# Reordering the passage, the batch change and every group of a fused attention and two-layer kernel

## The chip, the cores and the metric

One core of a Trainium2 chip. The metric is the device time of one execution in microseconds (us), the median over the runs that were timed. The engines are TensorE (PE in the profile, with PEld for its weight loads), VectorE (DVE), ScalarE (ACT), GpSimd (POOL) and SyncE (SP, which here issues the DMAs). Each runs its own instructions in the order in which they are written, and engines wait for one another by semaphores.

## What is computed

The reference, cut to what matters: masked attention, a first two-layer block with a squared ReLU, and a second block of four experts weighted for each token.

```python
mask = q_assign[:, :, :, None] == k_assign[:, :, None, :]
scores = np.where(mask, scale * np.matmul(q, k.transpose(0, 1, 3, 2)), -1e9)
attn = softmax(scores)                       # 2 batches, 8 heads, 768 x 768
x = np.matmul(attn, v)  ->  (1536, 512)
r = np.maximum(x @ w_in, 0.0)                # 512 -> 2048
x = (r * r) @ w_out                          # 2048 -> 512
p = domain_probs / (domain_probs.sum(-1, keepdims=True) + 1e-09)
for e in range(4):                           # 512 -> 1024 -> 512
    h = np.maximum(x @ w1[e], 0.0)
    out += p[:, e:e + 1] * (h @ w2[e])
```

Every operand of a product is held as a rounded part (`hi`) and a remainder (`lo`), and a product is three matmuls: hi by hi, hi by lo, lo by hi. So every weight and every activation is first rounded on ScalarE, and then its remainder is taken by a subtraction on VectorE or GpSimd.

## The kernel before

**Attention** fills the first 290 us of the profile and is not touched.

**The first block** runs over 48 iterations `n` = (4 chunks of 512 hidden columns) x (3 blocks of 512 tokens) x (4 tiles). Iteration `n` issues `gemm1(n)` (12 matmuls), `gemm2(n - 4)` (12 matmuls), and then what a list `plan` holds for slot `n`. ScalarE does ReLU, square and rounding of `gemm1`'s result (L636 to L638), GpSimd its remainder (L639). At the end of a block of tokens `gemm2`'s four banks are copied out by ScalarE (L653, first chunk) or added by VectorE (L655, later chunks). The slots of `plan` hold the conversions of the weights of coming chunks: five VectorE operations on the raw words (L161 to L177), then in the next slot the rounding on ScalarE (L183) and the remainder on VectorE (L185). `base` sets at which slot a chunk's conversions begin, `freed` when the raw buffer can be loaded again. The last slots prepare the second block: weight group 0 (`prep0`) and the first token operands.

**The second block** uses a Strassen-like scheme of 7 products for each 2 x 2 blocks. It runs over 32 groups `n`: 16 groups of 256 hidden columns (`NFQ`) for batch 0, and the same for batch 1. One group is 7 products (L756, 6 matmuls of 384 columns each) with 6 token tiles of the group before (L796, 6 matmuls of 512 columns each) between them. In each group:

- products 1, 6, 7 and 4 share PSUM bank A; before the next of them may write into it, ScalarE copies it out (`c_copy`, L767; product 6 waits for copy 0, product 7 for copy 1, product 4 for copy 2). Bank B or C is added to a copy on VectorE (`c_add`, L770).
- `h_hi` (ReLU and rounding, ScalarE, L776) and `h_lo` (remainder, VectorE, L779) make the operands of the next group's token tiles; VectorE adds each token tile's result to the output (L804, L806).
- `fq_prep(n + 1)` prepares the next group's weights in five steps: `sums` (four sums of 128x256 each, L715 to L718), `raws` and `mixed` (roundings L724, remainders L725), `second` (L742, L743), and the load of a later group.

**The token operands** are seven: RB11, RB21, RB22 straight from the first block's output, and RT1 to RT4, made of them by `t_sum` (L682). Each is rounded by `r_hi` (ScalarE, L685) and has its remainder by `r_lo` (VectorE or GpSimd, L688). For batch 0 this happens in **the passage** between the blocks, before group 0, and with the last `gemm2` calls put between group 0's products as `fill`. For batch 1 the four sums are all made in group 13, and the roundings and remainders in group 15, each after the product that used the old operand: **the batch change**.

The order on every engine is the order of this code; there is no scheduler.

Of the kernel before, what the change touches and what calls it, by code (L numbers as in the profile page):

```python
# [33 lines left out]
def moe_attention_kernel(  # L34
# [165 lines left out]
    with tc.manual_schedule():  # L200
# [502 lines left out]
        def fq_prep(n):  # L703
# [5 lines left out]
            def sums():  # L709
                w = st["r"] = raw_t["q", n][:, 0:1024].rearrange("p (k f) -> p k f", k=KD)  # L710
                a11, a12 = w[:, 0:2, 0:128], w[:, 2:4, 0:128]
                a21, a22 = w[:, 0:2, 128:256], w[:, 2:4, 128:256]
                s1, s2, s3, s4 = [mp["s"][:, k] for k in range(4)]
                sub = ALU.subtract
                nc.vector.tensor_tensor(s1, a21, a22, op=ALU.add)  # L715
                nc.vector.tensor_tensor(s3, a11, a21, op=sub)
                nc.vector.tensor_tensor(s2, s1, a11, op=sub)
                nc.vector.tensor_tensor(s4, a12, s2, op=sub)  # L718

# [24 lines left out]

            return [sums, raws, mixed, second, lambda: fq_load(n + 2)]

# [72 lines left out]
        for ci in range(NC1):  # L819
            base = 0 if ci == 0 else NF if ci == 1 else (ci - 1) * per  # L820
            for ci, part, half in w_loads(ci):
# [9 lines left out]
        for x in range(2):  # L831
            plan.append((freed[x - 2], 1, lambda x=x: fq_load(x)))
        prep0 = fq_prep(0)
        at0 = (NC1 - 1) * per
        for x, slot in ((0, at0), (1, at0 + 1), (2, at0 + 2), (3, at0 + LAG), (4, at0 + LAG)):
            plan.append((slot, 2, prep0[x]))
        plan.append((at0 + 2 * NF, 2, lambda: [r_hi(0, RB11), r_hi(0, RB21)]))
        plan.append((at0 + 2 * NF, 2, lambda: [r_lo(0, i, nc.gpsimd) for i in (RB11, RB21)]))
# [247 lines left out]
        for n in range(NEARLY, n1):  # L1086
# [6 lines left out]
                for k in range(2 * LAG)]  # L1093
        for i in (RT3, RT1):
            t_sum(0, i)
        r_hi(0, RT1)
        r_hi(0, RT3)
        t_sum(0, RT2)
        r_lo(0, RT1, nc.vector)
        r_hi(0, RT2)  # L1100
        r_lo(0, RT3, nc.gpsimd)
        t_sum(0, RT4)
        r_lo(0, RT2, nc.vector)
        r_hi(0, RT4)
        r_hi(0, RB22)
        r_lo(0, RB22, nc.gpsimd)
        r_lo(0, RT4, nc.vector)

        NN = 2 * NFQ
        for n in range(NN):  # L1110
            pb[n, "A"] = bank[n % 2]
            pb[n, "C"] = bank[2 + n % 2]
            pb[n, "B"] = bank[4] if n else bank[3]
            prep = fq_prep(n + 1)
            swap = n == NFQ - 1
# [6 lines left out]
            for x, i in enumerate(order):  # L1122
                product(n, i)
                if i == 1:
                    c_copy(n, 0)
                elif i == 6:
                    c_copy(n, 1)
                elif i == 2:
                    c_add(n, 0, "B")
                    h_hi(n, 0, 0)  # L1130
                elif i == 7:
                    c_copy(n, 2)
                elif i == 4:
                    h_hi(n, 1, 0)
                elif i == 3:
                    c_add(n, 1, "C")
                    h_hi(n, 0, 1)
                for f in fills[x]:
                    f()
                if i == 1 and n:  # L1140
                    h_lo(n - 1, 0, 1)
                elif i == 2:
                    h_lo(n, 0, 0)
                elif i == 7:
                    c_add(n, 2, "C")
                    h_hi(n, 1, 1)
                elif i == 4:
                    h_lo(n, 1, 0)
                    h_lo(n, 1, 1)
                if x < 5:  # L1150
                    prep[x]()
                if n == NFQ - 3 and x < 4:
                    t_sum(1, (RT3, RT1, RT2, RT4)[x])
                if swap:
                    r = PROD[i][1]
                    r_hi(1, r)
                    r_lo(1, r, nc.vector if x % 2 else nc.gpsimd)
        h_lo(NN - 1, 0, 1)
# [33 lines left out]
```

## Time and profile before

| | us |
|---|---|
| time, median of 3 runs | 1074.04 |
| lowest and highest run | 1072.1 and 1076.75 |
| the profiled execution | 1072.37 |
| span of its instructions | 1070.6 |
| TensorE busy | 1033.6 (97% of the span) |
| VectorE, ScalarE, GpSimd busy | 732.3, 538.2, 479.7 |

The profiled execution's time is 1.8 us above its span, and 1.7 us below the median of the runs. TensorE's busy time includes matmuls at the lower of its two clocks. A wait printed behind a row is the idle time of that engine just before the row, with the instruction that ended it.

### The profile page before, as it was taken

The numbers are of one execution on the slowest core, as the hardware profiler recorded it, in microseconds if no ns is written. First come the engines' busy times: TensorE is split into PE (matmuls) and PEld (weight loads), VectorE is DVE, ScalarE is ACT, GpSimd is POOL, SyncE is SP. The second block draws the span as 40 slices with busy tenths as digits, with TensorE's granted clock in tenths as the row PEclk, the third lists the DMA queues.
The fourth block names the chain that finished last, engine by engine and source line by source line (L and its number), as shares of the span: only waits on it lengthen the run. The fifth ranks groups of instructions, "written<-read, shape, count | busy, mean of one in ns | idle before, by whom it ended". The sixth has DMA issues, their size and how long they took to land.

```text
span 1070.6 us, 15323 instructions
## 1 busy us (share of the span) xinstructions
PE 1033.6 (97%) x5649; PEld 916.8 (86%) x5649; DVE 732.3 (68%) x1204; ACT 538.2 (50%) x1073; POOL 479.7 (45%) x465
## 2 busy tenths in 40 slices
PE   8899999998999999999989999999999999999998
PEld 7888888898887888888878888988888889989997
DVE  8698888787788873831156666666778666667664
ACT  6687887887655543434343333334344343333331
POOL 2467776665222222224343454444356454454440
PEclk9999999999999999999999999999999999999999
DMA  5766676873023230310002212211214212212201
GB/s 155 165 160 143 144 158 158 203 181 91 1 79 109 88 118 7 111 40 5 36 1 79 79 40 79 79 54 66 79 40 138 78 42 79 79 41 78 80 1 59
DMA packets 74651, 91.59 MB, mean 86 GB/s; under 512 B 27344, under 2 KB 50192, under 8 KB 74576
## 3 DMA queue, kind: packets, MB, share of 16 engines
q1 hardware_dynamic: 74576, 90.62, 29.7%
q8 instruction: 44, 0.72, 0.3%
q14 instruction: 31, 0.25, 0.1%
HBM read 59.83 MB, written 3.15 MB: 59 GB/s over the span
## 4 chain that ended last, share of the span: by engine, by line
PE 70%; DVE 6%; ACT 3%; DMA 2%; POOL 1%; issue 1%; SPq 0%; POOLq 0%; ACTq 0%
PE bank L796 23%; PE bank L756 20%; PE bank L649 10%; PE bank L631 3%; PE bank L632 3%; PE bank L630 3%; PE t L511 2%; PE s L478 1%; PE po L525 1%; PE po L527 1%; DVE ts L682 1%; PE m L377 1%; DVE x L806 1%; DMA q<-nql 0%; DVE fa L172 0%
## 5 line engine op out<-in xcount | busy, mean ns | idle before, releaser
L796 PE MATMUL bank<-w1h,ga 128*128 128x512 f32 x768 | 270.5, 394 | 0.0
L756 PE MATMUL bank<-xa,w0h 128*128 128x384 f32 x896 | 230.2, 338 | 8.4 <-ACT fa L767 8.4
L806 DVE SCALAR_TENSOR_TENSOR x<-bank,pe_p,x 128x512 f32<-128x512 f32 x180 | 134.7, 749 | 137.5 <-PE bank L796 137.5
L756 PEld LDWEIGHTS bank<-xa,w0h 128*128 128x128 f32 x896 | 164.9, 189 | 28.2 <-ACT fa L767 11.1
L796 PEld LDWEIGHTS bank<-w1h,ga 128*128 128x128 f32 x768 | 144.5, 188 | 24.6
L776 ACT ACTIVATE ga<-fa 128x384 fp32r<-128x384 f32 x96 | 50.4, 525 | 203.1 <-DVE fa L770 203.1
L796 PE MATMUL bank<-w1l,ga 128*128 128x512 f32 x384 | 151.9, 395 | 0.0
L756 PE MATMUL bank<-xa,w0l 128*128 128x384 f32 x448 | 150.5, 336 | 0.0
L639 POOL TENSOR_TENSOR ga<-fa,ga 128x512 fp32r<-128x512 f32 x48 | 63.0, 1313 | 189.7 <-ACT ga L638 132.6
L725 POOL TENSOR_TENSOR w0l<-raw,w0h 128x512 fp32r<-128x512 f32 x64 | 73.2, 1168 | 145.1 <-ACT w0h L724 145.1
L649 PE MATMUL bank<-ga,w1h 128*128 128x512 f32 x384 | 127.2, 391 | 2.2 <-ACT x L653 2.2
L517 DVE TENSOR_TENSOR ptl<-t,pth 128x384 fp32r<-128x384 f32 x192 | 99.1, 551 | 28.9 <-ACT pth L516 28.8
L725 POOL TENSOR_TENSOR w0l<-fa,w0h 128x1024 fp32r<-128x1024 f32 x32 | 77.3, 2415 | 76.2 <-ACT w0h L724 76.2
L487 DVE TENSOR_REDUCE nb<-s 128x1 f32<-128x768 f32 x96 | 91.2, 950 | 14.8 <-PE s L478 13.7
L767 ACT COPY fa<-bank 128x384 f32<-128x384 f32 x96 | 45.6, 475 | 105.2 <-PE bank L756 105.2
L516 ACT CAST pth<-t 128x384 fp32r<-128x384 f32 x192 | 83.1, 485 | 26.3 <-PE t L511 25.8
L743 POOL TENSOR_TENSOR w1l<-raw,w1h 128x1024 fp32r<-128x1024 f32 x32 | 85.4, 2668 | 21.5 <-ACT w1h L742 21.5
L511 PE MATMUL t<-identf,p 128*128 128x128 f32 x576 | 87.6, 279 | 6.3 <-DVE ptl L517 6.0
L498 ACT ACTIVATE p<-s,nb 128x768 f32<-128x768 f32 x96 | 87.5, 912 | 7.0 <-DVE nb L487 6.9
L478 PE MATMUL s<-k,q 80*128 80x384 f32 (+1 forms) x384 | 86.6, 346 | 2.7 <-DMA k<-ohm 2.5
L649 PEld LDWEIGHTS bank<-ga,w1h 128*128 128x128 f32 x384 | 72.5, 189 | 17.4 <-ACT x L653 2.6
L756 PEld LDWEIGHTS bank<-xa,w0l 128*128 128x128 f32 x448 | 84.7, 189 | 0.0
(180 smaller groups left out, 1997.1 us busy)
## 6 DMA issues: line engine op xcount, KB each, us to landing
raw<-in_moe_w_dram SPq DMA_DIRECT2D x64, 512.0 KB, 4.3
raw<-in_moe_w_in_dram SPq DMA_DIRECT2D x8, 1024.0 KB, 5.2
q<-nqh SPq DMA_DIRECT2D x42, 192.0 KB, 3.0
raw<-in_moe_w_out_dram SPq DMA_DIRECT2D x6, 1024.0 KB, 4.9
k<-nkh SPq DMA_DIRECT2D x28, 192.0 KB, 3.3
q<-nql SPq DMA_DIRECT2D x28, 192.0 KB, 3.7
nv<-in_v_dram SPq DMA_DIRECT2D x16, 192.0 KB, 3.7
out_dram<-x SPq DMA_DIRECT2D x12, 256.0 KB, 2.1
```

The lines of the kernel that those rows point to most:

```text
L478: nc.tensor.matmul(s[:, j, 0:HALF], stk[i, nq][:, t * 128:(t + 1) * 128], stk[i, nk][:, j * HALF:(j + 1) * HALF], start=first, stop=not first)
L487: nc.vector.tensor_reduce(out=nb, in_=s_ps[u][:, :, 0:HALF], axis=AX.XY, op=ALU.max, negate=True)
L498: nc.scalar.activation(p, s_ps.pop(u)[:, :, 0:HALF], AF.Exp, bias=nb_t.pop(u), accum_out=sums_t[hp][:, i % 2, t:t + 1])
L511: nc.tensor.transpose(tp[:, j], p_sb[u][:, half, j * 128:(j + 1) * 128], identf)
L516: return (lambda: nc.scalar.copy(dh, tp), lambda: nc.vector.tensor_tensor(dl, tp, dh.bitcast(F32), op=ALU.subtract))
L517: lambda: nc.vector.tensor_tensor(dl, tp, dh.bitcast(F32), op=ALU.subtract))
L649: nc.tensor.matmul(o, a, b, start=(ft == 0 and z == 0), stop=(ft == NF - 1 and z == 2))
L725: nc.gpsimd.tensor_tensor(v[1], src, v[0].bitcast(F32), op=ALU.subtract)
L743: nc.gpsimd.tensor_tensor(lo, w, hi.bitcast(F32), op=ALU.subtract)
L756: nc.tensor.matmul(ps, w[:, o:o + 128], r_op(r, x)[:, kt], start=(first and kt == 0 and z == 0), stop=(kt == 1 and z == 2), skip_group_che ...
L796: nc.tensor.matmul(o, a, w[:, f], start=(f == 0 and z == 0), stop=(f == 1 and z == 2))
L806: nc.vector.scalar_tensor_tensor(out=acc, in0=o, scalar=pc, in1=acc, op0=ALU.mult, op1=ALU.add)
```

## The change

No arithmetic is changed and TensorE's own order stays as it is. What other engines do is moved:

1. The conversions of chunks 1 to 3 of the first block begin two slots later.
2. The four weight sums of each group go from VectorE to GpSimd; `second` is issued before `mixed`.
3. `h_hi(n, 0, 0)` and `h_lo(n, 0, 0)` are issued after product 7 and its `c_copy`, no longer after product 2.
4. In the passage: the sums of group 1's weights are made before the passage, the token operands are written in a new order with part of them inside group 0's loop, their remainders all on VectorE, and the other preparation of group 1 begins at the third product.
5. The token sums of batch 1 are spread, one in each of groups 10 to 13. In group 15 the remainders are on GpSimd after the third and sixth product and else on VectorE (before: GpSimd and VectorE in turn, four and three).

```diff
-                nc.vector.tensor_tensor(s1, a21, a22, op=ALU.add)
-                nc.vector.tensor_tensor(s3, a11, a21, op=sub)
-                nc.vector.tensor_tensor(s2, s1, a11, op=sub)
-                nc.vector.tensor_tensor(s4, a12, s2, op=sub)
+                nc.gpsimd.tensor_tensor(s1, a21, a22, op=ALU.add)
+                nc.gpsimd.tensor_tensor(s2, s1, a11, op=sub)
+                nc.gpsimd.tensor_tensor(s3, a11, a21, op=sub)
+                nc.gpsimd.tensor_tensor(s4, a12, s2, op=sub)
...
-            return [sums, raws, mixed, second, lambda: fq_load(n + 2)]
+            return [sums, raws, second, mixed, lambda: fq_load(n + 2)]
...
-            base = 0 if ci == 0 else NF if ci == 1 else (ci - 1) * per
+            base = 0 if ci == 0 else NF + 2 if ci == 1 else (ci - 1) * per + 2
...
         prep0 = fq_prep(0)
+        prep1 = fq_prep(1)
         at0 = (NC1 - 1) * per
-        for x, slot in ((0, at0), (1, at0 + 1), (2, at0 + 2), (3, at0 + LAG), (4, at0 + LAG)):
+        for x, slot in ((0, at0), (1, at0 + 1), (3, at0 + 2), (2, at0 + LAG), (4, at0 + LAG)):
             plan.append((slot, 2, prep0[x]))
+        plan.append((at0 + LAG + 2, 2, prep1[0]))
...
-        for i in (RT3, RT1):
-            t_sum(0, i)
-        r_hi(0, RT1)
-        r_hi(0, RT3)
-        t_sum(0, RT2)
-        r_lo(0, RT1, nc.vector)
-        r_hi(0, RT2)
-        r_lo(0, RT3, nc.gpsimd)
-        t_sum(0, RT4)
-        r_lo(0, RT2, nc.vector)
-        r_hi(0, RT4)
-        r_hi(0, RB22)
-        r_lo(0, RB22, nc.gpsimd)
-        r_lo(0, RT4, nc.vector)
...
+        head = {
+            -1: [("t", RT3), ("t", RT1), ("h", RT1), ("t", RT2), ("l", RT1)],
+            0: [("h", RT2), ("h", RT3), ("t", RT4), ("l", RT2)],
+            1: [("l", RT3), ("h", RT4), ("h", RB22)],
+            2: [("l", RT4), ("l", RB22)]}
+        r_ops(0, head[-1])
...
                 elif i == 2:
                     c_add(n, 0, "B")
-                    h_hi(n, 0, 0)
                 elif i == 7:
                     c_copy(n, 2)
+                    h_hi(n, 0, 0)
...
-                elif i == 2:
-                    h_lo(n, 0, 0)
                 elif i == 7:
                     c_add(n, 2, "C")
+                    h_lo(n, 0, 0)
                     h_hi(n, 1, 1)
...
-                if x < 5:
-                    prep[x]()
-                if n == NFQ - 3 and x < 4:
-                    t_sum(1, (RT3, RT1, RT2, RT4)[x])
+                if n:
+                    if x < 5:
+                        prep[x]()
+                else:
+                    r_ops(0, head.get(x, []))
+                    if 2 <= x < 6:
+                        prep[x - 1]()
+                if x == 2 and 0 <= n - (NFQ - 6) < 4:
+                    t_sum(1, (RT3, RT1, RT2, RT4)[n - (NFQ - 6)])
                 if swap:
                     r = PROD[i][1]
                     r_hi(1, r)
-                    r_lo(1, r, nc.vector if x % 2 else nc.gpsimd)
+                    r_lo(1, r, nc.gpsimd if x in (2, 5) else nc.vector)
```

How this stands on the engines, at three places. First ScalarE in the first block's early iterations, before: the conversions' roundings (L183) stand between the steps of the iterations and ahead of the four copies L653.

```order
L183 CAST w0h<-cva 128x4x128
L636 ACTIVATE fa<-bank_4763 128x512
L637 ACTIVATE fa<-fa 128x512
L638 CAST ga<-fa 128x512
L183 CAST w0h<-fa 128x4x128
L636 ACTIVATE fa<-bank_4764 128x512
L637 ACTIVATE fa<-fa 128x512
L638 CAST ga<-fa 128x512
L653 COPY x_4769<-bank_4765 128x512
```

The same place after the change: the two roundings now come behind the copies.

```order
L636 ACTIVATE fa<-bank_4763 128x512
L637 ACTIVATE fa<-fa 128x512
L638 CAST ga<-fa 128x512
L636 ACTIVATE fa<-bank_4764 128x512
L637 ACTIVATE fa<-fa 128x512
L638 CAST ga<-fa 128x512
L653 COPY x_4769<-bank_4765 128x512
```

Second ScalarE in the passage, from RT1's rounding through group 0, before. `bank_4761` is bank A, `x_4769` and `ts` hold token operands, `w0h` and `w1h` group 1's weights.

```order
L685 CAST xa<-x_4769 128x768
L685 CAST xa<-ts 128x768 x3
L685 CAST xa<-x_4769 128x768
L767 COPY fa<-bank_4761 128x384
L776 ACTIVATE ga<-fa 128x384
L724 CAST w0h<-raw 128x512
L724 CAST w0h<-raw 128x256
L724 CAST w0h<-fa 128x1024
L767 COPY fa<-bank_4761 128x384
L742 CAST w1h<-raw 128x1024
L767 COPY fa<-bank_4761 128x384
```

After the change: the first copy stands behind one rounding in place of five, and no `h_hi` (L776) and no rounding of the weight sums (`fa`) stands ahead of the second copy.

```order
L685 CAST xa<-x_4769 128x768
L767 COPY fa<-bank_4761 128x384
L685 CAST xa<-ts 128x768 x3
L685 CAST xa<-x_4769 128x768
L724 CAST w0h<-raw 128x512
L724 CAST w0h<-raw 128x256
L767 COPY fa<-bank_4761 128x384
L742 CAST w1h<-raw 128x1024
L767 COPY fa<-bank_4761 128x384
L776 ACTIVATE ga<-fa 128x384 x2
L724 CAST w0h<-fa 128x1024
```

Third VectorE in one later group, from the second token tile's result on, before (L770 are the three `c_add`, L779 the `h_lo`).

```order
L806 SCALAR_TENSOR_TENSOR x_4769<-bank_4767,pe_p,x_4769 128x512
L806 SCALAR_TENSOR_TENSOR x_4769<-bank_4768,pe_p,x_4769 128x512
L770 TENSOR_TENSOR fa<-bank_4765,fa 128x384
L806 SCALAR_TENSOR_TENSOR x_4769<-bank_4766,pe_p,x_4769 128x512
L779 SCALAR_TENSOR_TENSOR ga<-fa,ga 128x384
L806 SCALAR_TENSOR_TENSOR x_4769<-bank_4767,pe_p,x_4769 128x2x256
L770 TENSOR_TENSOR fa<-bank_4763,fa 128x384
L806 SCALAR_TENSOR_TENSOR x_4769<-bank_4768,pe_p,x_4769 128x2x256
L779 SCALAR_TENSOR_TENSOR ga<-bank_4761,ga 128x384
```

After the change: the first `h_lo` has moved behind the second `c_add`, just ahead of the last token tile's result (the four sums ahead of these rows are gone).

```order
L806 SCALAR_TENSOR_TENSOR x_4769<-bank_4767,pe_p,x_4769 128x512
L806 SCALAR_TENSOR_TENSOR x_4769<-bank_4768,pe_p,x_4769 128x512
L770 TENSOR_TENSOR fa<-bank_4765,fa 128x384
L806 SCALAR_TENSOR_TENSOR x_4769<-bank_4766,pe_p,x_4769 128x512
L806 SCALAR_TENSOR_TENSOR x_4769<-bank_4767,pe_p,x_4769 128x2x256
L770 TENSOR_TENSOR fa<-bank_4763,fa 128x384
L779 SCALAR_TENSOR_TENSOR ga<-fa,ga 128x384
L806 SCALAR_TENSOR_TENSOR x_4769<-bank_4768,pe_p,x_4769 128x2x256
L779 SCALAR_TENSOR_TENSOR ga<-bank_4761,ga 128x384
```

## Rows read from the trace of the kernel before

**Rows 1.** The page's first part: busy us, share, instructions of each engine.
```profile
PE 1033.6 (97%) x5649; PEld 916.8 (86%) x5649; DVE 732.3 (68%) x1204; ACT 538.2 (50%) x1073; POOL 479.7 (45%) x465
```

**Rows 2.** TensorE's waits: us in total, times, longest.
```profile
PE bank L756 <- ACT fa L767: 8.4, 6, 3.4
```

**Rows 3.** TensorE's timeline, rows with a wait: start, us, idle before.
```profile
326.54 0.50 PE L649 MATMUL bank<-ga,w1h 128*128 128x512 f32 x1 [2.20 <-ACT x L653]
...
550.87 0.61 PE L756 MATMUL bank<-xa,w0h 128*128 128x384 f32 x2 [0.43 <-ACT fa L767]
557.02 0.97 PE L756 MATMUL bank<-xa,w0h 128*128 128x384 f32 x2 [3.43 <-ACT fa L767]
...
768.53 0.87 PE L756 MATMUL bank<-xa,w0h 128*128 128x384 f32 x2 [2.52 <-ACT fa L767]
...
803.04 0.62 PE L756 MATMUL bank<-xa,w0h 128*128 128x384 f32 x2 [1.41 <-ACT fa L767]
...
812.24 0.61 PE L756 MATMUL bank<-xa,w0h 128*128 128x384 f32 x2 [0.43 <-ACT fa L767]
...
820.03 0.62 PE L756 MATMUL bank<-xa,w0h 128*128 128x384 f32 x2 [0.23 <-ACT fa L767]
```

**Rows 4.** Windows: length, busy us (instructions) of each engine, granted clock, DMA.
```profile
557.09:560.50 3.41, 3.41 (x10) 3.12 (x11) 0.56 (x1) 1.33 (x3) 3.41 (x3) 0.50 0.00 0
560.50:563.91 3.41, 3.41 (x18) 3.02 (x17) 0.83 (x2) 1.00 (x2) 1.54 (x1) 1.00 0.17 44
768.71:772.13 3.42, 3.42 (x10) 3.10 (x11) 1.04 (x2) 1.01 (x2) 2.15 (x1) 0.50 0.02 6
```

**Rows 5.** ScalarE's timeline in the first block's iterations 6 to 8.
```profile
323.58 0.62 ACT L183 CAST w0h<-fa 128x512 fp32r<-128x512 f32 x1 [2.73 <-DVE fa L177]
...
325.91 2.04 ACT L653 COPY x<-bank 128x512 f32<-128x512 f32 x4
```

**Rows 6.** The passage, group 0: timelines of VectorE (first row) and ScalarE.
```profile
550.61 2.06 DVE L715 TENSOR_TENSOR fa<-raw 128x256 f32<-128x256 f32 x1
...
554.31 0.52 ACT L776 ACTIVATE ga<-fa 128x384 fp32r<-128x384 f32 x1 [3.49 <-DVE fa L770]
...
556.50 0.47 ACT L767 COPY fa<-bank 128x384 f32<-128x384 f32 x1
```

**Rows 7.** Groups 13 and 15: timelines of GpSimd, VectorE and ScalarE.
```profile
761.40 2.40 POOL L725 TENSOR_TENSOR w0l<-fa,w0h 128x1024 fp32r<-128x1024 f32 x1 [2.58 <-ACT w0h L724]
...
760.15 0.95 DVE L682 TENSOR_TENSOR ts<-x 128x768 f32<-128x768 f32 x1
...
761.68 2.94 DVE L682 TENSOR_TENSOR x<-x 128x768 f32<-128x768 f32 x1
...
766.64 0.52 ACT L776 ACTIVATE ga<-fa 128x384 fp32r<-128x384 f32 x1 [5.32 <-DVE fa L770]
...
797.76 1.05 ACT L724 CAST w0h<-fa 128x1024 fp32r<-128x1024 f32 x1 [1.81 <-DVE fa L718]
...
801.79 0.83 ACT L685 CAST xa<-x 128x768 fp32r<-128x768 f32 x1
```

**Rows 8.** Group 14, an undisturbed one: timelines of ScalarE, VectorE, GpSimd and TensorE.
```profile
780.24 1.05 ACT L724 CAST w0h<-fa 128x1024 fp32r<-128x1024 f32 x1
...
786.70 0.55 DVE L770 TENSOR_TENSOR fa<-bank,fa 128x384 f32<-128x384 f32 x1
...
788.47 0.75 DVE L806 SCALAR_TENSOR_TENSOR x<-bank,pe_p,x 128x512 f32<-128x512 f32 x1 [1.22 <-PE bank L796]
...
784.41 2.67 POOL L743 TENSOR_TENSOR w1l<-raw,w1h 128x1024 fp32r<-128x1024 f32 x1 [0.62 <-ACT w1h L742]
...
790.35 0.39 PE L796 MATMUL bank<-w1h,ga 128*128 128x512 f32 x1
```

**Rows 9.** GpSimd's cost: remainders of 512 and 256 columns, alone and over 31 groups.
```profile
555.41 1.95 POOL L725 TENSOR_TENSOR w0l<-raw,w0h 128x512 fp32r<-128x512 f32 x2 [3.02 <-ACT w0h L724]
...
L725 POOL TENSOR_TENSOR w0l<-raw,w0h 128x256 fp32r<-128x256 f32 x31 | 32.2, 1038 | 0.0
```

More of the change, by code (lines that the diff above doesn't have):

```diff
@@ L1093, in moe_attention_kernel, with r_ops @@
                 for k in range(2 * LAG)]
-        for i in (RT3, RT1):
-            t_sum(0, i)
-        r_hi(0, RT1)
-        r_hi(0, RT3)
-        t_sum(0, RT2)
-        r_lo(0, RT1, nc.vector)
-        r_hi(0, RT2)
-        r_lo(0, RT3, nc.gpsimd)
-        t_sum(0, RT4)
-        r_lo(0, RT2, nc.vector)
-        r_hi(0, RT4)
-        r_hi(0, RB22)
-        r_lo(0, RB22, nc.gpsimd)
-        r_lo(0, RT4, nc.vector)
+        def r_ops(b, ops):
+            for f, i in ops:
+                if f == "t":
+                    t_sum(b, i)
+                elif f == "h":
+                    r_hi(b, i)
+                else:
+                    r_lo(b, i, nc.gpsimd if f == "g" else nc.vector)
+        head = {
[4 more added lines that the diff above has]
+        r_ops(0, head[-1])
         NN = 2 * NFQ
@@ L1113, in moe_attention_kernel @@
             pb[n, "B"] = bank[4] if n else bank[3]
-            prep = fq_prep(n + 1)
+            prep = fq_prep(n + 1) if n else prep1
             swap = n == NFQ - 1
@@ L1149, in moe_attention_kernel @@
                     h_lo(n, 1, 1)
-                if x < 5:
-                    prep[x]()
-                if n == NFQ - 3 and x < 4:
-                    t_sum(1, (RT3, RT1, RT2, RT4)[x])
+                if n:
+                    if x < 5:
+                        prep[x]()
+                else:
+                    r_ops(0, head.get(x, []))
[3 more added lines that the diff above has]
+                    t_sum(1, (RT3, RT1, RT2, RT4)[n - (NFQ - 6)])
                 if swap:
```

## The prediction

> **What bounds the kernel now.** I read the page first: TensorE is busy for 97% of the span, the other engines for 45 to 68% [rows 1]. So the question is only where TensorE waits, and for whom. The view of its waits names one large group: six waits, 8.4 us together, of a product (L756) for ScalarE's copy of bank A (L767) [rows 2]. Its timeline then gives the place of each. After the attention it waits seven times, 2.20 + 0.43 + 3.43 + 2.52 + 1.41 + 0.43 + 0.23 = 10.65 us [rows 3]: once in the first block for the copies L653, twice in the passage (products 6 and 7 of group 0), once in group 13, once in group 15, twice in group 16. In all other groups it does not wait. The windows show that two of the waits, those of 3.43 and of 2.52 us, cost more than their length: behind each of them the granted clock is 0.50, the lower of the two levels (1.2 GHz), for 3.41 us, in which 10 matmuls start; in the 3.41 us after the first of these there are 18 at the full 2.4 GHz [rows 4]. That loses 3.41 x (1 - 10/18) = 1.5 us each time, 3.0 us for both. So what the change can win is at most 10.65 + 3.0 = 13.65 us, if it makes no new wait.
>
> **The first block, 2.20 us.** The four copies L653 run from 325.91 on; TensorE wants the banks from 326.54 - 2.20 = 324.34 on [rows 3, 5]. Just ahead of them ScalarE had waited 2.73 us for VectorE's conversion, then rounded for 0.62 us [rows 5]; two such roundings stand ahead of the copies, and the change puts both behind them. That frees 2 x (2.73 + 0.62) = 6.7 us on ScalarE against the 2.20 that are missing, so I count the wait as gone: **2.20**. What is late instead are the conversions of chunk 1. Its first weights are now rounded at slots 7 to 10 and first used in iteration 12, so a full iteration remains. The raw loads move with the slots, and no load passes another one on SyncE's queue. If that cover were gone, TensorE would wait at iteration 12 in place of iteration 8, and the term would be 0.
>
> **The passage, 3.86 us and one fall of the clock.** The 0.43 us before product 6 are its copy standing behind five roundings. Now it stands behind one; four roundings at 0.83 us [rows 7] are 3.3 us, so it goes. The 3.43 us before product 7 come from a chain: VectorE makes the sums for group 1, the first alone 2.06 us [rows 6]; behind them comes the `c_add` for which ScalarE's `h_hi` waits 3.49 us at 554.31; and behind that, after three weight roundings, comes the copy at 556.50 that TensorE needs [rows 6]. Of this chain the change removes each link: the sums are made before the passage, `h_hi` stands behind the copies, and only the short roundings of `raws` stand ahead of the second copy. Product 6 could start at 550.87 - 0.43 = 550.44; its six matmuls take 6 x 3.41 / 18 = 1.1 us at the full clock [rows 4], the copy 0.47, so it is there by 552.0, and TensorE reaches product 7 at 557.02 - 3.43 = 553.59 at the earliest [rows 3]. That leaves some 1.2 us, if the start moves 0.43 us forward too. VectorE gives up four sums and takes two more remainders of 0.95 us (the price of a sum of the same shape, [rows 7]). The last two remainders may meet GpSimd's `raws` remainders, 1.95 us for the pair [rows 9]; they serve the sixth and the seventh product only, two product and tile pairs away. So both waits go: **3.86**, and the lower clock behind them with them: **1.5**.
>
> **The batch change, 3.93 us and one fall.** In group 13 the second token sum begins at 761.68 and takes 2.94 us, where the first, of the same size, takes 0.95: GpSimd's 2.40 us remainder began at 761.40 and VectorE ends 0.8 us after it [rows 7]. The `c_add` behind it is late, ScalarE's `h_hi` waits 5.32 us for it [rows 7], the copy stands behind `h_hi`, and TensorE stands for 2.52 us. With one token sum in each of four groups and `h_hi` behind the copy, nothing that a copy waits for is behind a token sum any more: **2.52 + 1.5**. In group 15 the rounding of the mixed weights waits 1.81 us for the VectorE sums at 797.76 [rows 7], and further down the same line (behind the rounding at 801.79) is the copy for product 4; with the sums ready a group earlier on GpSimd the 1.41 us go: **1.41**. The two waits in group 16 (0.43 and 0.23) come from VectorE's and ScalarE's extra work for the new operands, which is the same work in another order. A gain there, or a wait up to twice as long, cannot be excluded; I leave them as they are, 0.66 us.
>
> **Each group, nothing.** Sums on GpSimd: a remainder of 512 with one of 256 columns takes 1.95 us undisturbed, so 0.65 us for 256; over the groups, against VectorE, the mean is 1.04 [rows 9]. Those are the two ends for one sum, 2.6 to 4.2 us a group. I take the lower, since the sums stand in a row behind the mixed remainder at the end of a group, where VectorE has few operations that read two operands from SBUF. GpSimd's work per group becomes 2.40 + 2.67 + 1.95 + 2.6 = 9.6 us [rows 7 to 9] of the group's 14.8 (78 matmuls at 3.41 / 18). To see whether that meets a need, I put the new order on group 14's clock [rows 8]. ScalarE rounds `second` at 780.24, then `mixed`, to 782.3. GpSimd's remainders run 2.67 us to 784.0 and 2.40 us to 786.4, and the four sums to 789.0. VectorE's second `c_add` ends at 787.25; behind it the moved `h_lo` may wait for one sum (0.65) and takes 0.55, so it ends by 788.5, when the last token tile's result at 788.47 is due. The next tile starts at 790.35. So there are 1.9 us of cover, and even at 1.04 for a sum nothing is late. With no cover each of 30 groups would pay what is missing.
>
> **The sum.** 2.20 + 3.86 + 1.5 + 2.52 + 1.5 + 1.41 = 13.0 us. The profiled execution took 1072.37 us for a span of 1070.6; it would become 1059.4. It lies 1.7 us below the median of the runs, 1074.04, which would become **1061.0**. Without a residue in group 16 it would be 1060.4.
>
> **Rivals.** (1) *A long wait stays at the batch change.* In group 15 five of the seven remainders are now on VectorE (three before), each 0.95 us, and up to 2.94 when GpSimd is at work [rows 7]. They stand ahead of `c_add`, `h_hi` and the next group's first copy. For it speaks that group 16 has its 0.43 us wait there already; against it that VectorE has lost four sums and that GpSimd has lost two remainders. With a wait like that of group 13, and its clock: 13.0 - 2.52 - 1.5 = 9.0, 1065.0.
> (2) *VectorE gets nothing for the sums it gives away*, because GpSimd holds it up just as long: the 2.94 for 0.95 us shows that it can [rows 7]. Then the two waits that had sums ahead of them, 3.43 with its clock and 1.41, stay in some form: 13.0 - 3.43 - 1.5 - 1.41 = 6.7, 1067.3. Against it: GpSimd makes them when VectorE mostly reads PSUM, and for the passage long before. The Trainium skill (Perfetto Trace Analysis, Optimizing Scalar/DVE Operations) speaks for this rival: it warns that handing work from one of the two to the other may not help, as they share a read port of SBUF; the trace agrees that they block each other, with that same 2.94 us.
> (3) *The shift of the conversions doesn't do what it says*: another operation keeps the copies L653 late, and 2.20 stay: 1063.2. Against it speak the 6.7 us freed.
> (4) *Slower.* The moved `h_lo` stands ahead of the last tile's result and of the operand that the next tile needs. If GpSimd's mixed remainder (2.40) and not one sum (0.65) runs when it is due, it ends at 787.25 + 2.40 + 0.55 = 790.2, the tile's result (0.75) and the next `h_lo` (0.55) at 791.5; the next tile, from 790.35 on [rows 8], wants that operand in its last matmul, 5 x 0.19 us on, at 791.3. From there on each group pays. At 13.0 / 30 = 0.43 us a group the gain is gone; at one more sum, 0.65 us, it is 1074.04 - 13.0 + 19.5 = 1080.5. Against it: `mixed` no longer waits for anything late, so it is done by 786.4.
>
> **How the numbers follow.** Forecast 0.62, rivals (1) 0.15, (2) 0.10, (3) 0.08, (4) 0.05. The likeliest gives 1061.0, by itself 1059 to 1063. The range reaches to 1067, which takes in (1), (3) and about half of (2), and down to 1058, for group 16's residue and medians that differ by some 2 us (runs: 1072.1 to 1076.75). A measurement of this kernel can tell about 0.5%, 5.4 us, from no change: faster is below 1068.7, the forecast, (1), (3) and half of (2), 0.90; the other half of (2) is within 0.5%, 0.05; (4) is slower, 0.05.
>
> **What would show it.** TensorE's waits for L767 fall from 8.4 us to under 1, the one for L653 is gone, the windows behind both long waits show granted clock 1.00, and the groups without token sums run as long as before. Four sums on GpSimd take 2.6 us, next to the mixed remainder. Wrong would be: a wait over 1 us in groups 15 or 16, any wait repeated in each group, or one at iteration 12 of the first block.

## The result and the profile after

The changed kernel takes 1061.45 us, the median of 4 runs from 1059.09 to 1062.48; the kernel before, run beside it, took 1073.07 (4 runs, 1071.6 to 1076.75). The ratio of the two times is 0.9884, with a 95% interval from 0.9853 to 0.9915, so the change is 1.2% faster. The profiled execution took 1061.5 us, with a span of 1059.7.

The page's first part for the changed kernel, to be read beside [rows 1]:

```profile
PE 1032.7 (97%) x5649; PEld 919.1 (87%) x5649; DVE 687.0 (65%) x1080; ACT 533.9 (50%) x1073; POOL 568.2 (54%) x589
```

VectorE is 45.3 us less busy and GpSimd 88.5 us more. TensorE's waits, the longest first:

```profile
PE m L437 <- POOL oh L411: 6.3, 7, 2.2
PE t L511 <- DVE ptl L517: 6.2, 6, 1.4
PE s L478 <- DMA k<-ohm: 2.2, 1, 2.2
```

All of these lie in the attention, which the change does not touch. The group of [rows 2] (L756 for L767, 8.4 us) and the wait for L653 are no longer in the list. The windows of the changed kernel (columns as in [rows 4]) show the same from the other side:

```profile
0.00:295.00 295.00, 272.13 (x2009) 254.38 (x2009) 239.17 (x437) 224.70 (x521) 166.00 (x282) 0.97 0.60 141
295.00:545.00 250.00, 250.00 (x1106) 207.07 (x1106) 131.61 (x206) 113.88 (x193) 78.13 (x62) 1.00 0.20 64
545.00:800.00 255.00, 255.00 (x1271) 229.09 (x1270) 167.31 (x222) 102.41 (x186) 170.33 (x127) 1.00 0.19 67
800.00:1059.00 259.00, 255.60 (x1269) 228.55 (x1267) 148.92 (x217) 92.90 (x174) 153.77 (x120) 1.00 0.19 66
```

From 295 us to 800 TensorE is never idle and the granted clock is 1.00; what is missing behind 800 is the end of the program. TensorE's own timeline: the end of the attention, two matmuls of the first block, product 7 of the passage, and the product of group 16 that had waited 0.43 us [rows 3]:

```profile
294.82 0.55 PE L590 MATMUL m<-rt,sel 24*128 24x128 f32 x3 [0.62 <-ACT rt L580]
...
324.71 0.39 PE L649 MATMUL bank<-ga,w1h 128*128 128x512 f32 x1
324.93 0.39 PE L649 MATMUL bank<-ga,w1l 128*128 128x512 f32 x1
...
554.82 0.51 PE L756 MATMUL bank<-xa,w0h 128*128 128x384 f32 x2
...
801.83 0.61 PE L756 MATMUL bank<-xa,w0h 128*128 128x384 f32 x2
```

The wait of 0.62 us at L590 is the last one printed in the program. Before, the same row stands at 290.21. It cuts the program in two: the attention ahead of it, and a **stretch** behind it that holds all that was changed. The stretch was 1070.6 - 290.21 = 780.4 us and is 1059.7 - 294.82 = 764.9, so the change gives **15.5 us** there. The attention, in the same code, is 4.6 us longer: its granted clock is 0.50 for 17.1 us, before for 6.8. The experiments are judged by the stretch for that reason. It is read from one profiled execution of each kernel; the four kernels of the table below that have no wait in it all show the same 764.9.

ScalarE's timeline in the first block, the passage and group 16, beside [rows 5, 6]:

```profile
325.43 2.04 ACT L653 COPY x<-bank 128x512 f32<-128x512 f32 x4
327.33 0.65 ACT L183 CAST w0h<-cva 128x512 fp32r<-128x512 f32 x1
...
553.68 0.48 ACT L767 COPY fa<-bank 128x384 f32<-128x384 f32 x1 [1.98 <-PE bank L756]
554.05 1.05 ACT L742 CAST w1h<-raw 128x1024 fp32r<-128x1024 f32 x1
...
801.31 0.47 ACT L767 COPY fa<-bank 128x384 f32<-128x384 f32 x1
```

The copies L653 stand ahead of the rounding. The copy for product 7 now waits for TensorE itself and ends at 554.16, 0.66 us before the product starts at 554.82. In group 16 it is close: the copy ends at 801.78, and the product starts at 801.83, some 0.1 us later than it could (its first two matmuls take 0.61 us, and 0.51 at 554.82). Last, GpSimd and VectorE in groups 9 and 10:

```profile
697.27 2.41 POOL L725 TENSOR_TENSOR w0l<-fa,w0h 128x1024 fp32r<-128x1024 f32 x1
699.76 0.74 POOL L715 TENSOR_TENSOR fa<-raw 128x256 f32<-128x256 f32 x1
700.58 0.74 POOL L716 TENSOR_TENSOR fa<-fa,raw 128x256 f32<-128x256 f32 x1
701.27 1.06 POOL L717 TENSOR_TENSOR fa<-raw 128x256 f32<-128x256 f32 x1
702.30 0.73 POOL L718 TENSOR_TENSOR fa<-raw,fa 128x256 f32<-128x256 f32 x1
...
710.54 2.41 POOL L743 TENSOR_TENSOR w1l<-raw,w1h 128x1024 fp32r<-128x1024 f32 x1 [2.54 <-ACT w1h L742]
711.04 2.73 DVE L682 TENSOR_TENSOR ts<-x 128x768 f32<-128x768 f32 x1
712.91 3.13 POOL L725 TENSOR_TENSOR w0l<-fa,w0h 128x1024 fp32r<-128x1024 f32 x1
```

The four sums stand next to the mixed remainder, at 0.73 to 1.06 us each. The token sum of group 10 takes 2.73 us in place of 0.95 [rows 7] and holds the remainder behind it (3.13 in place of 2.41): the two engines still block each other, but TensorE no longer waits for it.

### The profile page after: what moved, and what is told of

Read it like the earlier page. It is cut to its first block, busy times and chain, and to the rows that moved or that the text cites. A ratio compares the mean times of both kernels' runs of the same rounds, so it can differ in the third digit from the quotient of the medians.

```text
span 1059.7 us, 15269 instructions
## 1 busy us (share of the span) xinstructions
PE 1032.7 (97%) x5649; PEld 919.1 (87%) x5649; DVE 687.0 (65%) x1080; ACT 533.9 (50%) x1073; POOL 568.2 (54%) x589
## 4 chain that ended last, share of the span: by engine, by line
PE 78%; DVE 1%; DMA 1%; POOL 1%; ACT 1%; issue 0%; SPq 0%; POOLq 0%; ACTq 0%
PE bank L796 25%; PE bank L756 22%; PE bank L649 12%; PE bank L632 4%; PE bank L631 4%; PE bank L630 4%; PE t L511 2%; PE s L478 2%; PE po L527 1%; PE po L525 1%; PE m L377 1%; DMA q<-nql 1%; PE m L590 0%; PE s L630 0%; ACT p L498 0%
## 5 line engine op out<-in xcount | busy, mean ns | idle before, releaser
L756 PE MATMUL bank<-xa,w0h 128*128 128x384 f32 x896 | 228.5, 336 | 0.1
L756 PEld LDWEIGHTS bank<-xa,w0h 128*128 128x128 f32 x896 | 164.6, 188 | 17.8 <-ACT fa L767 0.5
L756 PE MATMUL bank<-xa,w0l 128*128 128x384 f32 x448 | 149.9, 335 | 0.0
L767 ACT COPY fa<-bank 128x384 f32<-128x384 f32 x96 | 45.5, 474 | 171.7 <-PE bank L756 171.7
L776 ACT ACTIVATE ga<-fa 128x384 fp32r<-128x384 f32 x96 | 50.5, 526 | 135.6 <-DVE fa L770 135.6
L743 POOL TENSOR_TENSOR w1l<-raw,w1h 128x1024 fp32r<-128x1024 f32 x32 | 77.2, 2413 | 71.4 <-ACT w1h L742 71.4
L779 DVE SCALAR_TENSOR_TENSOR ga<-fa,ga 128x384 fp32r<-128x384 f32 x96 | 90.2, 939 | 0.6 <-ACT ga L776 0.6
L636 ACT ACTIVATE fa<-bank 128x512 f32<-128x512 f32 x44 | 26.3, 598 | 118.1 <-PE bank L632 116.7
```

Of the source, the lines that this page charges most:

```text
L743: nc.gpsimd.tensor_tensor(lo, w, hi.bitcast(F32), op=ALU.subtract)
L756: nc.tensor.matmul(ps, w[:, o:o + 128], r_op(r, x)[:, kt], start=(first and kt == 0 and z == 0), stop=(kt == 1 and z == 2), skip_group_che ...
L779: nc.vector.scalar_tensor_tensor(out=g_t(n, f, t, 1), in0=h_src(n, f, t), scalar=0.0, in1=g_t(n, f, t, 0).bitcast(F32), op0=ALU.max, op1=A ...
```

## The experiments

The theory: TensorE waited for bank copies that stood in ScalarE's queue behind work that needed VectorE, and each part of the change takes such work out of the queue. The rivals: VectorE gets nothing back for the sums; a single part does nearly all of it; the longer GpSimd queue is a new bound close by. No kernel of the table leaves work out; those with the sums made twice and three times repeat them. "Idle" is the sum of TensorE's waits of 0.2 us and more in the stretch, "low" the time at clock 0.50 in the stretch ahead of its last 20 us.

| run | median us (runs) | ratio [95%] | attention us | stretch us | idle, low us |
|---|---|---|---|---|---|
| before (profiled) | 1072.37 (1) | | 290.21 | 780.4 | 10.65, 6.8 |
| after (profiled) | 1061.5 (1) | | 294.82 | 764.9 | 0, 0 |
| e1_conv_back | 1062.65 (4) | 0.9885 [0.9854, 0.9915] | 291.94 | 767.4 | 2.20, 0 |
| e2_sums_vector | 1061.77 (4) | 0.988 [0.9846, 0.9914] | 294.22 | 766.9 | 1.24, 0 |
| e3_token_sums_13 | 1060.85 (4) | 0.9859 [0.9832, 0.9886] | 293.89 | 765.5 | 0.41, 0 |
| e4_h_back | 1064.88 (4) | 0.9906 [0.9875, 0.9936] | 294.08 | 772.4 | 6.09, 0 |
| e5_only_h | 1075.38 (10) | 0.9989 [0.997, 1.0008] | 293.37 | 779.3 | 10.02, 6.8 |
| e6_passage_back | 1058.87 (1) | | 290.46 | 766.6 | 1.24, 0 |
| e7_sums_twice | 1057.08 (1) | | 290.40 | 764.9 | 0, 0 |
| e8_sums_thrice | 1087.44 (1) | | 292.74 | 792.9 | 18.9, 3.4 |
| e9_only_sums | 1069.34 (7) | 0.9948 [0.9929, 0.9967] | 292.04 | 774.5 | 6.76, 3.4 |
| e10_h_and_sums | 1064.58 (4) | 0.9903 [0.9878, 0.9927] | 291.26 | 771.4 | 3.81, 3.4 |
| e11_swap_back | 1055.01 (1) | | 288.37 | 764.9 | 0, 0 |
| e12_onehot_later | 1061.95 (4) | 0.9875 [0.9844, 0.9905] | 293.51 | 764.9 | 0, 0 |

**The conversions back at their old slots**, in the changed kernel:

```diff
-            base = 0 if ci == 0 else NF + 2 if ci == 1 else (ci - 1) * per + 2
+            base = 0 if ci == 0 else NF if ci == 1 else (ci - 1) * per
```

> The changed kernel with the conversions of chunks 1 to 3 back at their old slots, all else as changed. Measure: the stretch from the last L590 matmul group to the end of the span, 780.4 us before (290.21 to 1070.6) and 764.9 after (294.82 to 1059.7), which leaves the attention out. Each part its own wait: the wait of 2.2 us for the copies L653 returns and nothing else, with some 0.2 us for the restart: 767.3. Rival, the shift did nothing by itself: no wait there, 764.9.

TensorE's timeline has one wait in the stretch, the one of [rows 3]:

```profile
328.27 0.50 PE L649 MATMUL bank<-ga,w1h 128*128 128x512 f32 x1 [2.20 <-ACT x L653]
```

The stretch is 2.5 us longer. So this term is shown, and a wait of 2.20 us costs 2.5.

**The weight sums back on VectorE**, in the changed kernel:

```diff
-                nc.gpsimd.tensor_tensor(s1, a21, a22, op=ALU.add)
+                nc.vector.tensor_tensor(s1, a21, a22, op=ALU.add)
...
```

> The changed kernel with the four weight sums back on VectorE, all else as changed. The same stretch, 764.9 after. Each part its own wait: the moved order already took the sums out of the way of product 7 in the passage, so the 3.43 us stay away, but the sums delay VectorE in group 15 and the 1.41 us there return in whole or part: 765.5 to 766.5. Rival, relief of VectorE is the main thing: the passage's wait returns with its low clock too, 769 to 771. Second rival, the order alone does it: no wait at all, 764.9.

The stretch is 2.0 us longer, a little more than expected, with waits of 0.35 and 0.89 us; both lie in group 16, and none of 0.2 us or more comes back in group 15. GpSimd, VectorE, ScalarE and TensorE in the group behind the batch change:

```profile
805.00 2.49 POOL L743 TENSOR_TENSOR w1l<-raw,w1h 128x1024 fp32r<-128x1024 f32 x1
805.26 2.51 DVE L716 TENSOR_TENSOR fa<-fa,raw 128x256 f32<-128x256 f32 x1
...
808.48 1.05 ACT L724 CAST w0h<-fa 128x1024 fp32r<-128x1024 f32 x1 [3.56 <-DVE fa L718]
809.16 0.50 PE L796 MATMUL bank<-w1h,ga 128*128 128x512 f32 x1 [0.89 <-DVE x L806]
```

The sum L716 takes 2.51 us beside a GpSimd remainder of 2.49, where such a sum took 0.44 to 0.97 us on the mean of each line in the kernel before; a token tile's result behind it is late, and TensorE waits 0.89 us for its bank. So it does matter where the sums are made.

**The token sums back in group 13**, in the changed kernel:

```diff
-                if x == 2 and 0 <= n - (NFQ - 6) < 4:
-                    t_sum(1, (RT3, RT1, RT2, RT4)[n - (NFQ - 6)])
+                if n == NFQ - 3 and x < 4:
+                    t_sum(1, (RT3, RT1, RT2, RT4)[x])
```

> The changed kernel with the four token sums of batch 1 back in group 13, all else as changed. The same stretch, 764.9 after. Spreading is what counts: the four sums, each up to 2.7 us when GpSimd is at work, make the adds of bank C late and product 3 of group 13 waits 1 to 2.5 us, with the low clock at the upper end: 766 to 769. Rival, moving h_hi behind the copy was enough because no copy waits for a token sum any more: no wait, 764.9.

VectorE's second token sum and TensorE's only wait in the stretch:

```profile
760.82 2.04 DVE L682 TENSOR_TENSOR ts<-x,ts 128x768 f32<-128x768 f32 x1
...
764.04 0.62 PE L756 MATMUL bank<-xa,w0h 128*128 128x384 f32 x2 [0.41 <-DVE fa L770]
```

The stretch grows by 0.6 us, less than the theory's range. The token sums in group 13 still block, but with the other parts in place they hardly reach TensorE.

**The first `h_hi` and `h_lo` back behind product 2**, in the changed kernel:

```diff
                     c_add(n, 0, "B")
+                    h_hi(n, 0, 0)
                 elif i == 7:
                     c_copy(n, 2)
-                    h_hi(n, 0, 0)
...
+                elif i == 2:
+                    h_lo(n, 0, 0)
                 elif i == 7:
                     c_add(n, 2, "C")
-                    h_lo(n, 0, 0)
```

> The changed kernel with h_hi(n,0,0) and h_lo(n,0,0) back after product 2 in every group, all else as changed. The same stretch, 764.9 after. The move counts: in groups 10 to 13, where a token sum of 2.7 us stands ahead of the add of bank B, the copy for product 4 comes about 1 us later and product 4 waits up to 0.5 us in each, perhaps something in group 15 and the passage: 765.3 to 768. Rival, the spread alone is enough: no wait, 764.9.

This expectation failed: 772.4, or 7.5 us longer. Group 10 of this kernel shows how:

```profile
710.31 2.72 DVE L682 TENSOR_TENSOR ts<-x 128x768 f32<-128x768 f32 x1
...
713.53 0.53 ACT L776 ACTIVATE ga<-fa 128x384 fp32r<-128x384 f32 x1 [3.80 <-DVE fa L770]
713.96 1.03 ACT L724 CAST w0h<-fa 128x1024 fp32r<-128x1024 f32 x1
...
714.90 0.47 ACT L767 COPY fa<-bank 128x384 f32<-128x384 f32 x1
...
715.42 0.62 PE L756 MATMUL bank<-xa,w0h 128*128 128x384 f32 x2 [0.95 <-ACT fa L767]
```

The token sum is longer by the same 1.8 us as in the changed kernel (2.72 for 0.95), but now `h_hi` stands in ScalarE's queue for it, and behind it the rounding and the copy. This comes once in each of the four groups that hold a token sum (4 x 0.95), then 1.80 and 0.49 us come around the batch change. Spreading the token sums without moving `h_hi` makes four waits where there was one.

**Each of the two alone, and together**, in the kernel before. First only the move of `h_hi` and `h_lo`:

```diff
                     c_add(n, 0, "B")
-                    h_hi(n, 0, 0)
                 elif i == 7:
                     c_copy(n, 2)
+                    h_hi(n, 0, 0)
...
-                elif i == 2:
-                    h_lo(n, 0, 0)
                 elif i == 7:
                     c_add(n, 2, "C")
+                    h_lo(n, 0, 0)
```

> The kernel before with only the move of h_hi(n,0,0) and h_lo(n,0,0) behind product 7. The same stretch (from the last L590 group with a wait to the end), 780.4 before and 764.9 with the whole change. Theory, the place of h_hi on ScalarE was the main cause of the long waits: in group 13 the wait falls from 2.5 to under 0.5 with no low clock; in the passage h_hi no longer stands ahead of the second copy, but the rounding of the weight sums still does and waits for VectorE's sums, so product 7 waits 1.5 to 2.5 us in place of 3.4; group 15 keeps about 1; the 2.2 us of the first block stay. Stretch 770 to 773. Rival, the sums on VectorE are the main cause: both long waits stay over 2.5 us with their low clock, 779 to 780.

The rival held: 779.3, only 1.1 us less than before. ScalarE and TensorE in the passage, then VectorE and TensorE in group 13:

```profile
558.62 1.04 ACT L724 CAST w0h<-fa 128x1024 fp32r<-128x1024 f32 x1 [3.83 <-DVE fa L718]
559.57 0.47 ACT L767 COPY fa<-bank 128x384 f32<-128x384 f32 x1
560.09 0.88 PE L756 MATMUL bank<-xa,w0h 128*128 128x384 f32 x2 [3.38 <-ACT fa L767]
...
771.84 0.94 DVE L682 TENSOR_TENSOR ts<-x,ts 128x768 f32<-128x768 f32 x1
...
773.97 0.62 PE L756 MATMUL bank<-xa,w0h 128*128 128x384 f32 x2 [2.43 <-DVE fa L770]
```

In the passage the rounding of the sums took the place of `h_hi` ahead of the copy, with nearly the same wait. In group 13 the wait changed its releaser: no longer the copy L767, but VectorE's `c_add` itself (L770), which must read a bank before product 3 may write there. So VectorE's lateness reaches TensorE by two roads, through ScalarE's queue and directly, and to clear the first alone is worth little. Group 15's wait is gone here, but one of group 16 has grown from 0.43 to 1.59 us:

```profile
814.87 0.61 PE L756 MATMUL bank<-xa,w0h 128*128 128x384 f32 x2 [1.59 <-ACT fa L767]
```

Then only the sums on GpSimd, with `second` ahead of `mixed` (the diff's first two pieces, and in `prep0` the exchange of its steps 2 and 3); and last both:

> The kernel before with only the weight sums on GpSimd (and second ahead of mixed); h_hi where it was. The same stretch: 780.4 before, 764.9 with the whole change, 779.3 with only the move of h_hi. Theory now: VectorE's lateness reaches TensorE on two roads, through h_hi in ScalarE's queue to a copy, and through the add of bank C to product 3; so either edit alone shifts a wait and both together take it away. With the sums alone the road through h_hi stays open: group 13 still waits 1 to 2.5 us, group 15 about 2, the passage 1.5 to 3.5, the first block its 2.2: 773 to 778. Rival, the sums on GpSimd do it alone: no wait over 0.5 us after the first block's 2.2: 767 to 769.

> The kernel before with both: weight sums on GpSimd (second ahead of mixed) and h_hi, h_lo(n,0,0) behind product 7. Theory: far more than 1.1 us plus what the sums give alone. The first block keeps its 2.2 us, the passage 0.4 and 0.8 as with the passage put back, group 13 some 0.4 as with the token sums put back, group 16 at most 0.5, no low clock: 769 to 771. Rival, the edits add up without acting on each other: the waits of the passage and of group 13 stay over 1.5 us each: 773 or more.

The sums alone give 780.4 - 774.5 = 5.9 us, both together 9.0: more than 1.1 + 5.9. The last two kernels each hold one fall of the clock, 1.5 us, at a place where neither the kernel before nor the one after has it. The idle time, which leaves these falls out, says the same: it shrinks by 0.63 us with `h_hi`, 3.89 with the sums and 6.84 with both. With the sums alone the range of the theory held, though the passage waits 1.24 us in three waits and not 1.5 to 3.5. The fall of the clock lies in group 15 there, VectorE and TensorE:

```profile
796.90 3.14 DVE L688 TENSOR_TENSOR xa<-x,xa 128x768 fp32r<-128x768 f32 x1
...
801.22 0.88 PE L756 MATMUL bank<-xa,w0h 128*128 128x384 f32 x2 [2.32 <-DVE fa L770]
```

With both, the expected 769 to 771 were missed by 0.4 us, less than that fall; what is left are the waits of 2.20 (first block), 0.42 and 0.78 (passage) and 0.41 us (group 13), which are the other three parts' to remove.

**The passage as before**, in the changed kernel: the old block of `t_sum`, `r_hi`, `r_lo` ahead of group 0, the sums of group 1 and its other steps in group 0 as in any group.

```diff
-        plan.append((at0 + LAG + 2, 2, prep1[0]))
...
-        r_ops(0, head[-1])
+        for i in (RT3, RT1):
+            t_sum(0, i)
+        r_hi(0, RT1)
...
-                if n:
-                    if x < 5:
-                        prep[x]()
-                else:
-                    r_ops(0, head.get(x, []))
-                    if 2 <= x < 6:
-                        prep[x - 1]()
+                if x < 5:
+                    prep[x]()
```

> The changed kernel with the passage as before: token operands written in the old order ahead of group 0, group 1's sums made (on GpSimd) at the first product, preparation from the first product on. The same stretch, 764.9 after. Each part its own wait, and h_hi the main one: product 6 waits its 0.43 us again and product 7 up to 1 us, no low clock: 765.5 to 767. Rival, the passage's order is what took away its 3.43 us: these return with the low clock: 769 to 771.

ScalarE and TensorE there:

```profile
548.61 0.62 PE L756 MATMUL bank<-xa,w0h 128*128 128x384 f32 x2 [0.42 <-ACT fa L767]
...
553.09 1.05 ACT L724 CAST w0h<-fa 128x1024 fp32r<-128x1024 f32 x1 [2.38 <-POOL fa L718]
...
554.57 0.61 PE L756 MATMUL bank<-xa,w0h 128*128 128x384 f32 x2 [0.82 <-ACT fa L767]
```

0.42 and 0.82 us come back, not 0.43 and 3.43 with a fall of the clock: 1.7 us. The new order of the passage does the rest of what the sums on GpSimd and the move of `h_hi` have mostly done.

**The sums made twice, and three times**, on GpSimd, in the changed kernel (the four lines repeated, with the same result):

> The changed kernel with the four weight sums of each group made twice over on GpSimd (the same result): four more sums of 0.74 us a group. Same stretch, 764.9 after. Theory, there is cover: GpSimd goes from about 11.1 to 14.2 us of a group's 15.64, h_lo waits for one sum at most, no wait in the groups: 764.9 to 766. Rival (the slower case of the prediction): the longer row of sums holds h_lo and with it the next token tile, each group pays 0.3 us or more: over 774.

> The same with the sums three times over, eight more sums a group. Theory: GpSimd needs about 17.2 us a group and is the bound of groups of 15.64; some 29 groups pay about 1.6 us: 805 to 815, with waits of the products for the weights' remainders on GpSimd. Rival: GpSimd's printed spans overstate its work and there is still room: under 775.

Windows of one group (columns as in [rows 4]), with the sums made twice:

```profile
600.00:615.64 15.64, 15.64 (x80) 14.06 (x79) 9.84 (x13) 5.90 (x12) 13.29 (x13) 1.00 0.20 67
```

Three times:

```profile
841.34:857.71 16.37, 15.92 (x78) 13.99 (x79) 10.95 (x14) 6.00 (x12) 16.05 (x17) 1.00 0.19 66
```

A group is 15.64 us long before and after, and still with the second pass; GpSimd's busy time goes from 7.37 (before) to 10.28 (after) and 13.29 us. With another 3.0 us it would need 16.3, and there GpSimd is the bound: it is busy for 16.05 of 16.37 us, and TensorE waits 27 times for the copy behind the late rounding, 17.5 us together. At the end of that window, ScalarE and TensorE (L732 and L764 are L724 and L756 of the changed kernel):

```profile
856.23 1.05 ACT L732 CAST w0h<-fa 128x1024 fp32r<-128x1024 f32 x1 [3.72 <-POOL fa L726]
...
857.71 0.62 PE L764 MATMUL bank<-xa,w0h 128*128 128x384 f32 x2 [0.45 <-ACT fa L775]
```

Neither expectation met the size: 805 to 815 was too much, since a group grows only by what goes past 15.64 us, here 0.73, and the rival's under 775 was too little. So the changed kernel has room for one more pass of sums, 3.0 us a group, not for two.

**The remainders of the batch change in turn, as before**, in the changed kernel:

```diff
-                    r_lo(1, r, nc.gpsimd if x in (2, 5) else nc.vector)
+                    r_lo(1, r, nc.vector if x % 2 else nc.gpsimd)
```

> The changed kernel with the remainders of the batch change on GpSimd and VectorE in turn as before, all else as changed. The same stretch, 764.9 after. The prediction left group 16 its 0.66 us and the measurement has none: if the new division of the remainders is what took it away, 0.2 to 0.7 us come back there, 765.1 to 765.8; if the sums and h_hi did it, no wait, 764.9.

No wait, and the stretch is the same 764.9: this part of the change is worth nothing here. That this run's time is the lowest of the study, 1055.01, is the attention's doing (288.37 us, 3.4 us of it at clock 0.50).

**An attempt on the attention**: a table entry that makes the third head's one-hot operand one slot later, to move the wait of 2.2 us for it.

```diff
-'head': [[1, 2], [7, 8]]}
+'head': [[1, 2], [7, 9]]}
```

> The changed kernel with one number of the attention moved: the one-hot rows of the third head are put in place one step later (slot 9 in place of 8), where TensorE waits 2.2 us at 45.6 and the clock is low behind it for 3.4 to 6.8 us. Theory, GpSimd just needs the time: the wait shrinks below 1 us and no low clock follows: 3 to 5 us less in all executions. Rival, the scores that need these rows wait in its place for the rows to land: same time within 1 us.

The wait is still there, TensorE's timeline:

```profile
46.77 0.37 PE L437 MATMUL m<-identr,oh 128*64 128x128 f32 x3 [2.11 <-POOL oh L411]
```

The clock fell at 52.05 in place of 46.59, and was low for 10.2 us in the attention. The ratio's interval overlaps that of the changed kernel: no gain. None of the kernels tried has a shorter stretch than the changed one.

## Why the prediction was right, and where not

**All seven waits go: right.** So do both falls of the clock behind them; no place of [rows 3] has a printed wait now, and no new one came in their place, none at iteration 12 either. The cover was smaller than reckoned: counted from the wait at L590, the copies L653 begin 5.1 us sooner and not 6.7, and product 7's copy is 0.66 us early and not some 1.2. **A group without token sums runs as long as before: right** (15.64 us both times), although the prediction put a group at 14.8. Its pitch, 3.41 / 18, came from a window of [rows 4] in which 16 matmuls start and not 18; the other two had begun before it, at 559.92 and after. With 16 the group would come to 16.6, so that window is a poor ruler either way:

```profile
559.92 0.90 PE L649 MATMUL bank<-ga,w1h 128*128 128x512 f32 x2
560.65 0.40 PE L649 MATMUL bank<-ga,w1l 128*128 128x512 f32 x1
```

In the same way 9 and not 10 start in the window at clock 0.50. A fall then costs 3.41 x (1 - 9/16) = 1.5 us, as the prediction had it.

**The most that can be won, 13.65 us: too low.** The stretch gives 15.5. TensorE's order is the same in both kernels, so that each matmul's start can be set beside its own. From L590 on the changed kernel gains 2.50 us at the first block's wait, 0.71 and 5.28 at those of the passage, 4.34 in group 13, 1.84 in group 15, 0.32 and 0.50 in group 16, and nothing anywhere else. The 1.85 us above the prediction are some 0.26 us for each of seven waits, on the mean: the two matmuls behind a wait take 0.61 us [rows 3], without one 0.51, and the last one ahead of it takes its full 0.39 us, where in the flow the next starts 0.22 us later (324.71 and 324.93 above). The printed idle time leaves both out. The experiments agree: what the stretch has over 764.9, less the idle time and 1.5 us for each fall, is 0.3 us (1 wait) without the late conversions, 1.4 (6 waits) without the move of `h_hi`, 1.4 (5 waits) with that move alone, and 1.3 (6 waits) with the sums alone. Only with the sums back on VectorE is it more, 0.8 for two, where waits under 0.2 us are not in the count.

**Group 16's 0.66 us stay: wrong, they are gone.** The prediction put them down to the new operands' work, which only changes its order. The sums did it: with them alone on GpSimd no wait is left in group 16; with the move of `h_hi` alone there is one of 1.59 us, with the sums back on VectorE there are 0.35 and 0.89, and with the old division of the remainders none. The prediction's 13.0 for the stretch was 2.5 us short, by this term and by the cost of a wait, and the median still came within 0.5 us of its 1061.0. In the profiled execution the attention took 4.6 us back. That is no effect of the change: over the 14 profiled executions the attention ends between 288.37 and 294.82 us, also among kernels that do not differ there, and the time at clock 0.50 in it goes from 3.4 to 17.1 us with it. The medians scatter too: the kernel before, 1073.07 in the four runs beside the changed kernel, has 1076.49 (7 runs), 1076.1 (13) and 1076.01 (10) beside the experiments, and e12, with the changed kernel's stretch, is 14.1 us below the last of these. So the 0.5 us are luck; the 15.5 us of the stretch are not, though 3.0 of them hang on the two falls of the clock.

**Which part pays for which wait: in part wrong.** The prediction set down 2.52 + 1.5 us for group 13 to the spread and the move of `h_hi`, and group 15's 1.41 us to the sums. But without the spread only 0.41 us come back in group 13, while `h_hi` moved without the sums leaves 2.43 there; and with the sums alone another product of group 15 waits 2.32 us. For the 3.86 + 1.5 us of the passage it named the sums, `h_hi` and the new order together; the first two alone bring the waits there down to 1.20 and take away the fall. Taken back one by one, the stretch pays for the parts 2.5 (conversions), 2.0 (sums), 0.6 (spread), 7.5 (`h_hi`), 1.7 (passage) and 0 us (remainders of the batch change); added alone to the kernel before, the move of `h_hi` gives 1.1 and the sums 5.9. A link of the chain that is removed alone moves the wait to the next link, as in the passage and in group 13 with only `h_hi` moved. The exchange of `second` and `mixed` was never undone by itself, so the 5.9 us are those of the sums and the exchange together.

**The sums cost 0.65 us each on GpSimd: a little too low.** They take 0.76 to 0.97 on the mean of each line, some 3.25 us a group and not 2.6. There was cover for it: a second pass changes nothing.

**Rival (2), that VectorE gets nothing: half right, and harmless.** The four sums took VectorE 74.8 us before; it got back 45.3. The rest went into longer instructions elsewhere, above all `h_lo` (L779, from 784 to 939 ns on the mean of 96, 14.9 us) and the token sums (3.5 us), and into the four remainders that VectorE now makes in GpSimd's place (3.8 us at 0.95). The Trainium skill (Perfetto Trace Analysis, Optimizing Scalar/DVE Operations) warns that handing work between these two engines might not help, and the trace agrees on the blocking, with a token sum of 2.73 us for 0.95. Yet here it helped: the sums' move is worth 2.0 us to the whole and 5.9 alone, and the longer instructions make TensorE wait nowhere. **Rival (1)** did not come, though group 16's copy comes so late that some 0.1 us is lost; **rival (3)** did not come; a wait in each group, as in **rival (4)**, begins only between the second and the third pass of sums, and by another road (the rounding of the sums; for `h_lo` TensorE waits there only once, 1.6 us).

## What to carry to other kernels

When an engine in a chain of in-order queues is late, follow every road from it to the bound engine before you move one instruction: clearing one road can leave the wait in place under another releaser's name, as in group 13. Judge such a change by the part of the program that it touches, between two rows that both traces have, and not by the whole time, when another part scatters by more than the effect. Count what a wait costs from the start of the matmul ahead of it to the pace behind it, not by its printed idle time alone.

## What the runs showed of the hardware

The same wait need not bring the same clock. The first block's 2.20 us wait stands in five kernels; behind it the granted clock stayed at 1.00 in four (before, and e1, e5, e9), and fell to 0.50 in one, e10. The window right behind that wait, in the kernel before:

```profile
326.60:330.01 3.41, 3.41 (x15) 2.83 (x16) 2.69 (x4) 2.61 (x6) 0.82 (x1) 1.00 0.35 143
```

The same in e10:

```profile
328.71:332.11 3.40, 3.40 (x10) 2.63 (x9) 2.62 (x6) 2.57 (x5) 0.00 (x0) 0.50 0.05 19
```

Runs of one kernel scatter with the granted clock: ten runs of the kernel before, in one sitting, go from 1071.35 us at a mean clock of 0.993 to 1077.64 at 0.987. The 0.006 between them are 0.012 of the span at half speed, some 13 us, of which 1.5 in 3.41 is lost by the reckoning above: 5.7 us, most of the 6.3 between the two runs. In between the order is rough: of these runs one of 1075.8 us has a clock of 0.988 and one of 1077.53 has 0.989.
